# Gated linear attention and a gated feed-forward on one core: wider array tiles for nine chunks, twelve products fewer, another written order

## The chip, the cores and the metric

The kernel runs on one core of a Trainium2 chip. The metric is device time in microseconds (us), the median over runs. The engines are TensorE (PE, with its weight loads shown apart as PEld), VectorE (DVE), ScalarE (ACT), GpSimd (POOL) and SyncE (SP), which only issues transfers here. Each engine works through its own instructions in the order in which the program lists them and waits where an input isn't there.

## The reference

```python
# q, k, v, f_logit: (4, 8, 768, 48)   batch, head, time, head_dim
f = 1.0 / (1.0 + np.exp(-f_logit))
for t in range(S):
    state = f[:, :, t, :, None] * state + np.einsum('bhd,bhe->bhde', k[:, :, t], v[:, :, t])
    y[:, :, t] = np.einsum('bhd,bhde->bhe', q[:, :, t], state)
x = y, heads side by side                      # (4, 768, 384)
h = np.maximum(x @ w_in, 0.0)                  # 384 -> 1024
conv = sum over k of conv_w[k] * h shifted by k - 1 in time
out = (h * sigmoid(conv)) @ w_out              # 1024 -> 384
```

The attention is a linear recurrence with a decay per row of the state. The feed-forward takes its output, convolves the hidden layer over three steps in time for a gate, and projects back.

## The kernel before

**Chunks.** Time is cut into chunks of 128, six per batch, 24 in all; chunk n is batch n // 6. The eight heads stand as four pairs, one head on partitions 0 to 47 and one on 64 to 111. In a chunk the recurrence becomes products. Two exponentials of the summed gate logarithm (`decays`, tile fi and fd) scale k and q (`scaled_k`, `scaled_q`). `scores` multiplies them into a 128x128 triangle per head (PSUM tile pa) and DVE copies it under a mask (am). `turned` transposes k (ptk, then kp). `state` forms the rank update of the state from kp and v (pk) and decays the state. `values` adds the masked scores times v and the old state times q (py), and writes a high and a low half for the feed-forward (xT). Products in plain fp32 leave two records each in the trace, one for each pass.

**Scores and rank updates.** `scores` (L328) cuts the triangle into 32-row strips and leaves out the part above the diagonal: for each pair and each strip two products, one per head, with 48 rows and 32 weight columns; the moving side is 128, 96, 64 or 32 columns long. That is 32 products per chunk. `state` (L343) cuts each head's update in two halves of 32 columns: 16 products per chunk, with 128 rows, 32 weight columns and 64 moving columns. The last chunk of a batch has no update.

**Feed-forward.** It works on half batches of 384 time steps (unit u), in single-pass products (fp32r) of high and low halves: three per pair of blocks. `hidden` makes one of eight blocks of 128 hidden channels: 9 products into ph, ACT and DVE for the gate's argument; `gated` the gate; `result` splits 128 rows into gh and gl (ACT L468, DVE L470) and makes 24 products into po. The weights come as 64-bit numbers and are turned into high and low halves on the chip by POOL, ACT and DVE (`single`, `split`).

**The order.** Nothing is scheduled by a program. Every function is a generator that yields after each step, and the string ORDER (L25 to L78) names which generator makes its next step. A token's letter is the function: F, L, M, V load gate logarithms, k, q and v (SP); x is the gate (ACT, twice), G its sum (PE for the first six chunks, DVE later), p the decays (ACT), t the last decay (POOL), K and Q the scaled k and q, a the scores (PE, then DVE's mask), k the transpose (PE, then ACT), s the update (PE, DVE, POOL), y the values (PE, PE, ACT, DVE). I and O load weights, J and P widen them, H and S split them; c is the convolution's weights; h, m and j are the hidden layer, r the result, z and b a closing check. Behind the letter is the chunk, the block or unit and block. For one engine only the order of its own steps counts, so the order of a token among those of other engines matters through the waits alone. SP's loads stand in one queue as well: a load that waits for its buffer holds back those behind it. The gate logarithms have two buffers of three chunks (tag "fb"), so F6 to F8 wait for G0 to G2.

**Zero products.** `warm` (L528) is token w: 12 products of 512 columns in fp32r, from two places of the split weights that are set to zero at the start (L164 to L166), into a PSUM buffer that nothing reads. In the order they stand around r0.0 to r0.2:

```
S7 S7 m2.4 j1.4 j1.4 m1.6 m2.4 m2.4 m1.6 h2.4 m2.5 G11 r0.0 r0.0 r0.1 V12 r0.0 m2.4 r0.0 s9 r0.0 w w y9 s9 p11 w w s9
r0.0 m1.7 p11 w x12 w w w w w Q11 y9 a10 m1.1 m2.7 w m1.0 r0.1 L12 r0.1 r0.1 r0.1 m1.7 m1.1 K11 j1.6 m1.1 m1.0 r0.2 j1.6
V11 m2.7 m2.7 y10 m2.7 j1.0 s10 y10 a11 r0.2 w y10 s10 m2.6 h2.6 m2.6 m2.5 j1.0 r0.1 m2.0 M12 m2.2 r0.2 y10 m2.1 m2.0
```

(An r token makes its casts and subtractions first and then a quarter of its products at each of four further tokens.)

Of the kernel before, what the change touches and what calls it, by code (L numbers as in the profile page):

```python
# [30 lines left out]
J1.1 K4 P3 p5 k3 O5 J1.1 t4 H2.1 J1.1 m0.0 m0.3 K5 P0 G6 Q4 m0.0 P3 y3 p5 m0.3 F11 y3 h0.2 M5 F9 P3 m0.1 H1.1 m0.1 y3 M6  # L31
P0 p6 V6 L7 m0.0 P3 s3 K6 P3 M7 H0.1 H0.1 s3 P5 m0.1 s3 P0 V4 O2 P0 a4 m0.2 m0.2 m0.2 H1.1 a4 h0.4 m0.6 m0.0 S3 p7 y3
m0.1 S3 m0.3 k4 x8 m0.0 m0.1 P0 m0.2 F10 x8 m0.3 k4 P0 Q5 m0.6 p6 P2 K7 G8 a5 t6 m0.5 m0.5 x9 s4 y4 s4 m0.2 P5 x9 Q6
m0.5 y4 m0.4 y4 m0.5 m0.4 P5 a5 S0 m0.6 m0.2 m0.1 y4 k6 O1 P2 a6 m0.4 S0 m0.3 m0.6 m0.5 s4 P2 y5 t5 y5 p8 O6 P5 P5 m0.4
k6 m0.5 P5 m0.7 y5 m0.7 m0.7 m0.1 k7 m0.2 M8 y5 p7 Q7 m0.4 t7 P2 P1 k7 M10 m1.1 m1.0 a6 j0.2 s6 m0.0 p8 m0.5 O4 t8 S5 P2
M9 j0.0 y6 m1.0 G9 m1.1 P1 L8 m0.4 s6 y6 j0.0 m0.7 m1.1 a7 m1.2 m0.7 h1.0 m1.1 P1 m1.2 a7 m1.2 m1.4 F12 Q8 P2 m0.4 y6
m0.6 K8 m0.6 P1 V7 m1.0 m1.4 j0.4 y7 L9 k8 m1.0 S2 m1.5 y7 m1.5 p9 j0.4 L11 j0.2 L10 G10 S5 P4 F14 F13 h1.2 P4 k8 m1.4
K9 h1.4 m1.2 s7 x12 p9 m0.6 m1.5 m1.3 m1.4 V8 m1.3 m1.3 t9 a8 m1.7 P1 m1.5 m0.7 P1 m0.7 L13 m1.6 m1.3 P6 y7 P4 s7 m1.6
S1 P4 k9 P4 m1.5 m1.6 k9 s7 j0.6 m1.2 O7 a8 m1.7 p10 y7 s8 S2 j0.6 P4 K10 y8 Q9 y8 m1.3 s8 m1.7 h1.6 a9 y8 y8 m1.7 m1.7
P7 m1.2 k10 m2.3 P6 m1.2 m1.3 P6 m2.2 S1 m1.6 P7 k10 m2.3 V9 P7 m1.3 p10 r0.0 P6 P6 j1.2 m2.3 m2.5 a9 s8 m1.6 t10 S4 P6  # L40
m1.0 j1.2 r0.0 S4 P7 m2.3 V10 m2.2 m1.4 m1.4 P7 m1.4 M11 m1.5 m2.5 m2.2 h2.2 m2.5 Q10 S6 y9 P7 m2.2 y9 r0.1 m1.5 a10 S6
S7 S7 m2.4 j1.4 j1.4 m1.6 m2.4 m2.4 m1.6 h2.4 m2.5 G11 r0.0 r0.0 r0.1 V12 r0.0 m2.4 r0.0 s9 r0.0 w w y9 s9 p11 w w s9
r0.0 m1.7 p11 w x12 w w w w w Q11 y9 a10 m1.1 m2.7 w m1.0 r0.1 L12 r0.1 r0.1 r0.1 m1.7 m1.1 K11 j1.6 m1.1 m1.0 r0.2 j1.6
V11 m2.7 m2.7 y10 m2.7 j1.0 s10 y10 a11 r0.2 w y10 s10 m2.6 h2.6 m2.6 m2.5 j1.0 r0.1 m2.0 M12 m2.2 r0.2 y10 m2.1 m2.0
m2.0 G13 m2.6 G14 m2.1 F15 m2.7 r0.2 p13 K13 t11 k13 m2.1 m2.3 m2.6 r0.5 m2.6 r0.2 r0.2 G12 h2.0 M13 r0.2 r0.2 m2.7 p13
k13 s10 p12 m2.1 p12 r0.5 a11 V13 m2.4 Q13 L14 y11 Q12 y11 K12 a12 m2.0 m2.3 m2.4 r0.5 r0.4 t13 r0.2 r0.4 r0.5 V14 r0.4
F17 F16 y11 r0.5 m2.5 M14 p14 r0.5 r0.4 m2.1 x15 m2.3 y11 x15 k12 r0.1 m3.2 r0.3 p14 t12 k12 K14 m2.7 a12 a13 M15 m2.6
m2.2 m2.1 r0.2 r0.5 m2.2 r0.3 L15 m2.4 y12 s12 m2.0 m3.2 j2.2 m2.1 m2.0 s12 j2.2 r0.4 r0.4 m2.0 L16 k14 m3.3 y12 j2.0
m3.2 r0.4 V15 G15 m2.6 G16 h3.2 p15 k14 m2.5 m3.0 j2.0 m3.3 t14 m3.3 m3.0 M16 m3.2 K15 m3.0 s13 m3.1 m3.1 s13 j2.6 s13
a13 y12 m3.2 h3.0 m3.1 m3.0 k15 m3.3 m3.3 p16 F19 m3.6 K16 m3.6 k15 m3.5 p15 m3.2 G17 m3.6 m3.1 m3.1 Q14 m3.5 m3.5 s14  # L50
j2.4 m3.1 j2.6 r0.5 m3.0 y13 j2.4 h3.6 m3.6 y13 y13 h3.4 p16 a14 s14 a14 r1.0 F20 k16 m3.7 y13 m3.5 r0.3 m3.7 k16 r1.0
Q16 F18 m3.6 L17 m3.7 m3.7 Q15 y14 s15 x18 s14 m3.1 y14 m3.7 m3.5 m3.2 r0.4 a15 r1.0 t15 r1.0 V18 y14 r0.3 m3.7 m3.7 x18
V17 a15 s15 m3.5 m3.4 m3.4 G18 m3.4 r0.3 m3.6 p17 r1.0 r0.3 m3.5 s15 r1.0 M17 p17 m3.4 y14 r1.1 m3.0 K17 m3.0 r0.3 t16
y15 m3.3 L18 r1.0 F23 j3.0 r1.1 F21 V16 m3.4 M19 s16 y15 a16 m3.6 y15 Q17 s16 p18 r1.1 r1.1 a16 K18 m3.4 r1.1 m3.4 r0.3
p18 y15 j3.0 r1.1 m3.3 m4.4 k18 j3.6 F22 m4.7 m4.7 G19 r1.1 m4.5 m4.5 L19 j3.4 m4.4 m4.7 p19 y16 y16 j3.2 a17 j3.4 t17
K19 j3.6 r1.1 m4.4 m4.5 r1.0 s16 h4.6 k18 m4.7 a17 h4.4 m4.4 r1.2 k19 m4.5 y16 j3.2 k19 y16 m4.1 m4.0 t18 h4.0 m4.0 G20
r1.2 h4.2 M18 m4.0 m4.3 m4.1 m4.1 m4.0 m4.1 m4.3 V19 Q18 y17 p19 r1.2 s18 r1.3 r1.3 r1.2 x21 M20 y17 y17 m4.4 a18 L20
m4.6 m4.2 L21 m4.5 Q19 m4.3 m4.6 m4.6 m4.4 x21 a18 m4.2 s18 t19 y17 m4.0 m4.2 s19 m4.0 y18 m4.3 y18 m4.2 y18 G23 a19
m4.3 m4.3 m4.0 m4.6 s19 L22 r1.2 r1.2 m4.5 r1.3 r1.2 m4.2 G21 r1.2 r1.5 r1.3 V22 p20 m4.6 m4.5 r1.2 m4.2 m4.2 r1.3 p20
r1.3 t20 m4.7 r1.3 r1.4 r1.2 M23 r1.5 r1.5 m4.1 m4.4 j4.4 K20 r1.5 Q20 p21 m4.6 m4.6 r1.5 p21 a19 r1.5 m5.5 m4.1 m5.5  # L60
r1.4 m5.5 m4.1 m4.3 r1.5 r1.5 m5.4 r1.3 K21 y19 t21 j4.0 j4.4 y19 a20 p23 k20 j4.0 p23 s19 m5.4 m5.4 M21 L23 r1.4 m4.7
m4.7 j4.2 r1.4 j4.2 Q21 h5.4 k20 a20 r1.4 j4.6 j4.6 m5.4 V20 m5.4 m5.5 r1.4 m5.5 r1.4 m5.7 m5.4 m5.7 m5.1 K23 r2.0 m5.1
m5.1 m5.7 m5.3 m5.3 h5.6 y19 m5.3 r2.0 r2.1 k21 y19 m5.4 m5.7 h5.0 r1.4 m5.0 m5.0 h5.2 m5.0 m5.5 m5.1 k21 m5.3 m5.6 m5.6
m5.3 m5.2 G22 m5.2 m5.2 m5.6 p22 m5.7 m5.0 r2.0 y20 m5.7 m5.3 m5.5 m5.7 m5.0 r2.1 s20 s20 M22 y20 j5.4 a21 m5.6 r2.0 V21
m5.3 r2.1 y20 m5.6 y20 j5.4 a21 t23 m5.6 s20 r2.0 m5.0 m5.0 r2.0 p22 Q22 m5.6 r2.1 j5.6 j5.6 r2.1 K22 r2.1 h6.6 s21 m5.1
m5.1 m5.2 h6.4 y21 t22 y21 Q23 r2.1 m5.2 a22 r2.0 r2.2 m6.4 m6.5 s21 m6.1 m5.2 m6.4 r2.0 m5.2 m6.4 m6.5 m5.1 m6.1 m6.5
j5.2 a22 s21 j5.0 j5.0 m6.4 h6.0 m6.6 z m6.6 k22 m6.5 m6.1 y21 r2.2 m6.0 m6.1 j5.2 m6.0 m6.6 m6.7 r2.2 r2.5 m6.7 m6.7
m6.4 k22 r2.2 m6.4 y21 m6.5 m6.0 y22 m6.4 m6.5 m6.5 s22 y22 m6.6 r2.5 a23 s22 r2.2 y22 m6.6 m6.6 r2.2 r2.1 r2.2 r2.2 a23
m6.1 m6.0 m6.7 m6.7 r2.5 r2.3 s22 r2.5 m6.1 y22 m6.2 V23 r2.2 m6.3 r2.5 m6.0 m6.1 j6.4 m6.7 m6.0 r2.5 m6.0 r2.4 j6.0
r2.3 m6.3 m6.2 m6.3 m6.7 m6.2 h6.2 m6.6 r2.5 j6.6 y23 m6.3 j6.0 y23 y23 y23 r2.3 j6.4 m6.3 r2.3 m6.2 m6.3 r2.2 r2.3 j6.6  # L70
r2.3 m6.2 r2.3 m6.3 m7.7 h7.6 m6.2 m7.1 m7.1 z m7.7 m7.7 m7.1 m7.0 h7.0 m7.7 m7.0 r2.4 m7.2 m7.1 m7.1 m7.0 m7.2 m7.1
m7.0 m7.4 m7.0 r2.3 m7.2 h7.4 m7.4 m7.4 m6.2 j6.2 m7.4 j6.2 m7.5 h7.2 m7.1 m7.5 m7.2 m7.2 m7.2 m7.0 m7.0 m7.4 m7.5 m7.4
m7.3 m7.3 m7.7 m7.6 m7.6 m7.3 m7.5 m7.7 r3.0 r3.0 m7.6 m7.3 m7.3 r2.4 m7.5 j7.0 m7.7 r2.4 r2.4 m7.6 m7.3 m7.5 r2.4 m7.5
m7.3 r3.0 r3.1 m7.4 m7.2 r3.0 r3.1 j7.2 j7.2 r3.0 r2.5 m7.6 r3.0 r3.1 r3.0 r3.0 r3.2 j7.0 r3.1 r2.4 r3.1 m7.6 r3.2 r3.2
m7.6 r3.2 r3.1 r3.2 r3.2 r3.2 j7.4 r3.2 r3.2 r3.2 z r3.2 j7.4 r3.2 j7.6 j7.6 r3.1 r3.2 z r3.2 r3.2 r3.2 r3.2 r3.2 r3.2
# [6 lines left out]
def gla_moe_kernel(ctx, tc, q_in, k_in, v_in, f_in, w_in, conv_w, w_out, out):  # L82

    nc = tc.nc
# [243 lines left out]
    def scores(n):  # L328
        kT, qT = raw["k", n], raw["q", n]
        for p in range(NP):  # L330
            for i in range(NB):
# [9 lines left out]
        yield
# [364 lines left out]
```

## Time and profile before

| | us |
|---|---|
| median of the runs shown | 317.6 |
| the runs | 317.25, 317.6, 320.34 |
| the profiled execution | 316.99 |
| its span | 315.3 |
| PE busy | 301.2 (96%) |
| DVE busy | 255.7 (81%) |
| ACT busy | 225.9 (72%) |
| POOL busy | 74.8 (24%) |

The span runs from the first to the last instruction of one execution. Times in the rows are counted from the start of the span. An engine's busy time adds up its instructions; for PE the end of each product is modelled, so a PE that is always busy may still have stalls in it, and what a product takes is read from one start to the next.

### The profile page before, as it was taken

To read this page: it belongs to the slowest core of one execution; us is meant where nothing else is said; L and a number is where in the kernel's file an instruction comes from. 1 tells how busy PE (TensorE), PEld (TensorE's weight loads), DVE (VectorE), ACT (ScalarE), POOL (GpSimd) and SP (SyncE) were. 2 spreads that over 40 slices of the span, in tenths; PEclk is the share of its full clock that TensorE was granted. 3 is DMA by queue.
4 is the path that set the end of the run, shared out by engine and by line. 5 is a ranking of instruction groups with operands and counts; after the bars stand their busy time and mean duration, and the time that the engine had idled before them with its cause. 6 is when DMAs were issued, how large, how long until landed. Compare 5 with 4: busy or idle time off the path is not lost.

```text
span 315.3 us, 10904 instructions
## 1 busy us (share of the span) xinstructions
PE 301.2 (96%) x4747; PEld 276.6 (88%) x4747; DVE 255.7 (81%) x389; ACT 225.9 (72%) x424; POOL 74.8 (24%) x106
## 2 busy tenths in 40 slices
PE   6887899999999999999999999999999999999995
...
PEclk9699999999999999999999999999999999999998
...
GB/s 240 364 282 349 379 266 37 152 266 22 202 4 92 176 154 93 120 201 68 38 166 121 160 71 4 58 152 94 2 0 87 2 27 0 52 1 0 78 52 53
DMA packets 19382, 36.93 MB, mean 117 GB/s; under 512 B 2156, under 2 KB 5252, under 8 KB 19332
## 3 DMA queue, kind: packets, MB, share of 16 engines
...
q8 instruction: 38, 0.62, 0.7%
...
q14 instruction: 12, 0.10, 0.1%
...
## 4 chain that ended last, share of the span: by engine, by line
PE 90%; DMA 3%; ACT 3%; issue 2%; SPq 1%; DVE 1%
PE po L482 32%; PE ph L429 32%; PE py L373 11%; PE pa L336 6%; PE pk L351 3%; PE ptk L321 3%; PE pl L285 2%; DMA fb<-in_f_logit_dram 2%; DMA v<-in_v_dram 1%; PE pz L531 1%; DVE g L450 1%; ACT fb L267 1%; ACT g L448 1%; ACT L448 0%; SPq L259 0%
## 5 line engine op out<-in xcount | busy, mean ns | idle before, releaser
L429 PE MATMUL ph<-xT,wih 128*128 128x384 f32 x384 | 101.8, 345 | 2.5 <-issue 1.5
L429 PEld LDWEIGHTS ph<-xT,wih 128*128 128x128 f32 x384 | 67.1, 188 | 6.4 <-issue 4.2
L482 PE MATMUL po<-woh,gh 128*128 128x384 f32 x192 | 65.0, 339 | 0.0
L429 PE MATMUL ph<-xT,wil 128*128 128x384 f32 x192 | 64.5, 336 | 0.0
L482 PE MATMUL po<-woh,gl 128*128 128x384 f32 x192 | 64.2, 335 | 0.0
L482 PE MATMUL po<-wol,gh 128*128 128x384 f32 x192 | 64.2, 334 | 0.0
L439 DVE SCALAR_TENSOR_TENSOR g<-hb,cw,g 128x384 f32<-128x384 f32 (+1 forms) x64 | 42.1, 669 | 12.9 <-ACT g L437 12.8
L470 DVE TENSOR_TENSOR gl<-g,gh 128x1024 fp32r<-128x1024 f32 (+4 forms) x34 | 31.8, 942 | 12.4 <-ACT gh L468 12.1
L441 DVE SCALAR_TENSOR_TENSOR g<-hb,cw,g 128x384 f32<-128x384 f32 (+1 forms) x64 | 40.7, 652 | 0.5
L432 ACT ACTIVATE hb<-ph 128x384 f32<-128x384 f32 x64 | 30.8, 488 | 13.8 <-PE ph L429 13.7
L437 ACT ACTIVATE g<-hb,cw 128x384 f32<-128x384 f32 (+1 forms) x64 | 38.8, 615 | 0.5
L482 PEld LDWEIGHTS po<-woh,gh 128*128 128x128 f32 x192 | 36.0, 188 | 0.7 <-issue 0.2
L468 ACT CAST gh<-g 128x1024 fp32r<-128x1024 f32 (+4 forms) x34 | 26.7, 804 | 13.2 <-PE po L482 13.1
L482 PEld LDWEIGHTS po<-wol,gh 128*128 128x128 f32 x192 | 36.1, 188 | 0.1
L429 PEld LDWEIGHTS ph<-xT,wil 128*128 128x128 f32 x192 | 36.0, 188 | 0.0
L482 PEld LDWEIGHTS po<-woh,gl 128*128 128x128 f32 x192 | 36.0, 188 | 0.0
L315 POOL TENSOR_TENSOR q<-q,fd 128x512 f32<-128x512 f32 x19 | 26.7, 1406 | 35.8 <-ACT fd L300 21.1
L339 DVE COPY_PREDICATED am<-mask,pa 128x1024 f32<-128x1024 uint8 x24 | 31.9, 1327 | 4.0 <-PE pa L336 3.9
L450 DVE SCALAR_TENSOR_TENSOR g<-g,hb 128x768 f32<-128x768 f32 (+1 forms) x32 | 31.2, 985 | 4.6 <-ACT g L448 4.5
L448 ACT ACTIVATE g<-g 128x768 f32<-128x768 f32 (+1 forms) x32 | 26.9, 844 | 8.9 <-DVE g L441 8.6
L361 POOL TENSOR_TENSOR st<-st,ft_all 128x256 f32<-128x256 f32 x16 | 14.1, 883 | 72.1 <-DVE st L359 72.1
L373 PE MATMUL py<-am,v 128*32 128x128 f32 x768 | 26.5, 280 | 0.1
...
## 6 DMA issues: line engine op xcount, KB each, us to landing
...
```

Of the source, the lines that this page charges most:

```text
L315: (nc.vector if n < QV else nc.gpsimd).tensor_tensor(raw["q", n], raw["q", n], fds[n][1], ALU.mult)
L339: nc.vector.copy_predicated(a_b[n % 2].rearrange("p j (x y) t -> p (j x) y t", y=2), mask, pa.rearrange("p j (x y) t -> p (j x) y t", y=2))
L373: nc.tensor.matmul(py[G * p:G * p + G, t, :], lhs, rhs, start=start, stop=stop)
L429: nc.tensor.matmul(ph, w, xts[b, hf][:, t, xl, :], start=(k == 0), stop=(k == 3 * KT - 1))
L432: nc.scalar.activation(hb[:, 2:HS + 2], ph, AF.Relu, scale=0.5)
L437: nc.scalar.activation(cv, hb[:, 1:n + 1], AF.Copy, scale=cw[:, 1, f:f + 1])
L439: nc.vector.scalar_tensor_tensor(cv, hb[:, 2:n + 2], cw[:, 2, f:f + 1], cv, ALU.mult, ALU.add)
L441: nc.vector.scalar_tensor_tensor(cv, hb[:, 0:n], cw[:, 0, f:f + 1], cv, ALU.mult, ALU.add)
L448: nc.scalar.activation(cv, cv, AF.Tanh)
L450: nc.vector.scalar_tensor_tensor(cv, cv, 1.0, h_b[:, fp:fp + 2, 1:n + 1], ALU.add, ALU.mult)
L470: nc.vector.tensor_tensor(lo, g[:, f:f + k], hi.bitcast(F32), ALU.subtract)
L482: nc.tensor.matmul(po, g[:, f, :], w, start=(i == 0), stop=(i == 3 * NF - 1))
```

## The change

Four edits. For chunks below NA = 9, `scores` makes one product per pair and head: 48 rows, 128 weight columns, 128 moving columns, the whole square, 8 products per chunk. For the same chunks, `state` makes one product per pair and head: 128 rows, 64 weight columns, 64 moving columns, 8 per chunk. Token w, its generator and the two memsets are gone. ORDER is written anew; apart from w it has the same tokens, each as often as before.

```diff
+NA = 9
...
 ORDER = """
-F0 I0.0 F1 c J0.0 x0 x0 L0 G0 M0 x1 F2 I1.0 J0.0 J0.0 p0 x1 L1 V0 c G1 L2 p0 c J0.0 c J0.0 K0 Q0 x2 c c p1 J0.0 a0 c M1
-x2 a0 p1 K1 I2.1 H0.0 k0 F3 c G2 k0 t0 I2.0 H0.0 y0 F7 p2 J1.0 s0 M2 y0 J1.0 J1.0 x3 Q1 J1.0 F4 K2 J1.0 x3 s0 c V1 a1
-J1.0 t1 a1 p2 k1 J2.0 t2 F5 Q2 G3 y0 I0.1 k1 J2.0 x7 x7 k2 k2 s1 J2.0 y0 H1.0 G7 p3 V2 y1 x4 J2.1 J2.1 s1 J2.0 J2.1 J2.0
-H1.0 F6 a2 I1.1 L3 J2.0 y1 y1 x4 p3 J2.1 H2.0 a2 M3 G4 J0.1 J2.1 y1 O3 y2 s1 K3 O0 Q3 J0.1 J2.1 h0.0 x6 J1.1 L4 J0.1 x5
-J0.1 H2.0 L6 s2 F8 y2 a3 y2 s2 J0.1 s2 x5 y2 t3 L5 h0.6 J0.1 H2.1 V3 p4 p4 a3 G5 m0.3 x6 J1.1 m0.0 k3 M4 P3 V5 J1.1 m0.3
...
+F0 x0 I0.0 F1 L0 x0 M1 x1 J0.0 J0.0 J0.0 G0 p0 F3 x1 p0 J0.0 c c J0.0 M0 G1 K0 c L1 c F2 p1 I1.0 Q0 V0 x2 J0.0 J1.0 k0 c
+x2 k0 c H0.0 J1.0 K1 L2 a0 p1 c c J1.0 a0 H0.0 I2.0 G2 t0 y0 p2 J1.0 Q1 J1.0 y0 I2.1 p2 c x3 K2 M2 F7 x3 J1.0 t2 s0 a1
+s0 H1.0 J2.0 V1 F4 J2.1 I0.1 a1 y0 J2.0 k1 k1 F5 G3 Q2 k2 h0.6 L4 J2.1 x7 V2 M3 J2.0 x7 y0 H1.0 x4 k2 y1 J2.0 t1 J2.0 L3
+I1.1 V3 y1 F8 G7 s1 J2.0 J2.1 J2.1 J2.1 J0.1 F6 s1 y1 x4 O0 p3 y1 p3 H2.0 a2 O3 a2 K3 J0.1 O5 s2 s1 M5 Q3 V4 x5 J0.1 G4
+y2 J2.1 J0.1 H2.0 s2 y2 y2 J0.1 a3 x5 M4 y2 H2.1 p4 J1.1 k3 k3 L5 J1.1 H2.1 x8 t3 J0.1 K4 a3 G5 x6 O2 p4 O6 J1.1 x6 J1.1
...
+m2.4 r0.0 j1.4 S6 S7 m1.7 m1.0 j1.4 M11 r0.1 G11 r0.0 M13 r0.0 r0.0 m1.7 m2.5 m1.6 h2.4 m2.4 r0.0 m2.4 t10 r0.0 r0.1 t9
+r0.2 m1.1 m1.0 r0.2 r0.1 m1.1 p11 m1.6 m1.7 p11 x12 y9 r0.1 s9 s9 r0.1 m1.0 m2.7 r0.1 m2.1 y9 m2.1 a10 m2.1 m2.7 j1.0
...
 """
...
-    WARM = 12
...
-    wz, wy = wih[:, KT - 1, DFF - WC:], woh[:, NF - 1, :P]
-    nc.gpsimd.memset(wz.bitcast(F32), 0.0)
-    nc.gpsimd.memset(wy.bitcast(F32), 0.0)
...
     def scores(n):
         kT, qT = raw["k", n], raw["q", n]
-        for p in range(NP):
+        for p in range(NP if n < NA else 0):
+            for j in range(2):
+                r = slice(HP * j, HP * j + D)
+                nc.tensor.matmul(pa[:, j, p, :], kT[r, p, :], qT[r, p, :], start=True, stop=True)
+        for p in range(NP if n >= NA else 0):
             for i in range(NB):
...
         for p in range(NP):
             for j in range(2):
+                if n < NA:
+                    nc.tensor.matmul(pk[HP * j:HP * j + HP, p, :], kp[:, 2 * p + j, :], vt[:, p, j, :],
+                                     start=True, stop=True)
+                    continue
                 for x in (0, G):
...
-    def warm():
-        for i in range(WARM):
-            pz = ps.tile([P, WC], F32, tag="mm", name=f"pz{i}", bufs=MB)
-            nc.tensor.matmul(pz, wy, wz, start=True, stop=True)
-            yield
-
-    todo = {"c": load_cw(), "z": checked(), "b": loaded(), "w": warm()}
+    todo = {"c": load_cw(), "z": checked(), "b": loaded()}
```

On PE, the order of the first chunks changes from G0 G1 a0 k0 c G2 y0 s0 y0 a1 k1 G3 k2 s1 y1 a2 y1 G4 y2 s2 y2 a3 G5 to G0 G1 k0 a0 c G2 y0 y0 s0 a1 k1 G3 k2 y1 y1 s1 a2 s2 G4 y2 y2 a3 k3 G5. From r0.0 on it was r0.0 s9 w (ten) m2.7 w r0.1 m2.7 m2.7 y10 and is, with s9 now ahead, r0.0 m2.4 r0.1 m2.7 m2.1.

## Rows read from the trace of the kernel before

**Rows 1.** Page, the span in 40 slices: PE and the granted clock, in tenths.
```profile
PE   6887899999999999999999999999999999999995
...
PEclk9699999999999999999999999999999999999998
```

**Rows 2.** Windows: us, length, busy PE, PEld, DVE, ACT, POOL, clock, DMA share, GB/s.
```profile
88.00:96.00 8.00, 8.00 (x153) 7.47 (x153) 8.00 (x14) 6.57 (x13) 0.44 (x1) 1.00 0.02 4
...
104.00:112.00 8.00, 8.00 (x182) 7.43 (x182) 6.96 (x11) 6.32 (x12) 1.26 (x1) 1.00 0.53 179
```

**Rows 3.** Timeline of PE around the zero products (pz): start, length, group, count.
```profile
99.07 2.58 PE L531 MATMUL pz<-wih,woh 128*128 128x512 f32 x10
101.49 0.51 PE L429 MATMUL ph<-xT,wih 128*128 128x384 f32 x2
...
102.01 0.40 PE L531 MATMUL pz<-wih,woh 128*128 128x512 f32 x1
102.25 0.33 PE L482 MATMUL po<-woh,gh 128*128 128x384 f32 x1
...
110.42 0.50 PE L531 MATMUL pz<-wih,woh 128*128 128x512 f32 x1
110.75 0.51 PE L429 MATMUL ph<-xT,wih 128*128 128x384 f32 x2
```

**Rows 4.** Timeline of DVE: the subtraction that r0.1's products need.
```profile
98.68 1.20 DVE L470 TENSOR_TENSOR gl<-g,gh 128x1024 fp32r<-128x1024 f32 x1
```

**Rows 5.** Timeline of PE: update, values, scores, transposes of one chunk.
```profile
80.29 0.65 PE L351 MATMUL pk<-v,kp 128*32 128x64 f32 x32
80.76 1.06 PE L373 MATMUL py<-am,v 128*32 128x128 f32 x32
...
83.07 1.00 PE L336 MATMUL pa<-q,k 48*32 48x128 f32 x64
84.00 0.66 PE L321 MATMUL ptk<-ident,k 128*128 128x128 f32 x4
84.41 0.59 PE L429 MATMUL ph<-xT,wih 128*128 128x384 f32 x2
```

**Rows 6.** Timeline: full 128x128 fp32 products of G4 and their loads; the scores' loads.
```profile
26.09 0.97 PEld L285 LDWEIGHTS pl<-tri,fb 128*128 128x128 f32 x8 [1.44 <-ACT fb L267]
26.09 1.16 PE L285 MATMUL pl<-tri,fb 128*128 128x128 f32 x8 [1.17 <-ACT fb L267]
...
83.06 0.80 PEld L336 LDWEIGHTS pa<-q,k 48*32 48x32 f32 x64 [0.25 <-POOL mswo L180]
```

**Rows 7.** Timeline of PE: the rows with idle time put down to issue.
```profile
29.07 0.37 PE L351 MATMUL pk<-v,kp 128*32 128x64 f32 x12 [0.55 <-issue]
...
35.97 0.51 PE L429 MATMUL ph<-xT,wih 128*128 128x384 f32 x2 [0.82 <-issue]
...
42.30 0.63 PE L336 MATMUL pa<-q,k 48*32 48x64 f32 x40 [0.53 <-issue]
...
48.69 0.45 PE L429 MATMUL ph<-xT,wih 128*128 128x384 f32 x1 [0.67 <-issue]
```

**Rows 8.** Windows between and after those stops, and one early stretch; columns as in rows 2.
```profile
29.07:35.90 6.83, 5.70 (x127) 4.94 (x127) 6.83 (x12) 6.22 (x14) 4.77 (x7) 1.00 1.01 371
...
42.30:48.68 6.38, 5.72 (x127) 4.92 (x127) 6.02 (x11) 6.38 (x13) 3.38 (x3) 1.00 0.62 221
48.68:55.00 6.32, 6.31 (x155) 5.00 (x160) 5.03 (x8) 4.12 (x9) 4.50 (x7) 1.00 0.16 47
...
10.20:16.00 5.80, 5.80 (x98) 4.93 (x101) 4.41 (x9) 3.97 (x9) 1.75 (x4) 0.50 0.84 332
```

**Rows 9.** Timeline: ACT ahead of G4's products, and G5's products.
```profile
25.02 0.48 ACT L401 CAST xT<-py 128x384 fp32r<-128x384 f32 x1 [0.63 <-PE py L373]
...
31.26 1.16 PE L285 MATMUL pl<-tri,fb 128*128 128x128 f32 x8 [0.38 <-ACT fb L267]
```

**Rows 10.** Timeline of PE: G1's products, ahead of the stretch at half clock.
```profile
8.89 1.42 PE L285 MATMUL pl<-tri,fb 128*128 128x128 f32 x8 [1.87 <-ACT fb L267]
```

More of the change, by code (lines that the diff above doesn't have):

```diff
@@ L31 @@
[L31 to L75, printed above, removed]
@@ new lines @@
+I1.1 V3 y1 F8 G7 s1 J2.0 J2.1 J2.1 J2.1 J0.1 F6 s1 y1 x4 O0 p3 y1 p3 H2.0 a2 O3 a2 K3 J0.1 O5 s2 s1 M5 Q3 V4 x5 J0.1 G4
+y2 J2.1 J0.1 H2.0 s2 y2 y2 J0.1 a3 x5 M4 y2 H2.1 p4 J1.1 k3 k3 L5 J1.1 H2.1 x8 t3 J0.1 K4 a3 G5 x6 O2 p4 O6 J1.1 x6 J1.1
+p5 m0.3 m0.3 m0.3 s3 F11 P3 J1.1 s2 G6 P3 J1.1 P0 K5 V6 p5 m0.3 h0.0 m0.0 s3 P3 P3 h0.2 m0.0 Q4 H1.1 y3 H0.1 m0.1 h0.4
+P0 x8 P3 m0.1 m0.2 p6 y3 L6 k4 m0.0 t4 H0.1 F10 m0.2 m0.1 H1.1 P0 P3 K6 m0.0 m0.4 a4 P0 O1 m0.0 m0.2 S3 P0 a4 k4 m0.1 p7
+F9 P5 m0.5 P5 y3 P5 Q5 M6 L7 x9 P5 y3 P5 m0.3 S3 p6 m0.4 m0.5 a5 s3 P0 G8 s4 V5 P2 m0.5 Q6 s4 m0.4 y4 m0.1 V7 t6 m0.4
@@ new lines @@
+m0.2 x9 a5 m0.1 L8 K7 y4 m0.6 y4 y4 S0 p8 m0.5 P2 G9 m0.6 m0.5 k6 s4 m0.6 O4 m0.2 S0 M7 y5 y5 m0.0 y5 m0.5 m0.4 a6 P5 y5
+m0.7 m0.7 m0.6 k6 k7 t5 L9 m0.0 p7 m1.1 L10 m0.1 S5 a6 m0.3 k7 m0.5 m1.1 P2 m1.1 m0.2 P1 j0.0 m0.7 S5 p8 m1.0 Q7 m0.7
+j0.0 m0.7 s6 P2 t8 P1 y6 y6 m0.4 s6 M9 a7 P2 a7 M8 m1.0 h1.0 m1.1 m1.0 t7 m0.2 m1.0 m0.3 m1.3 m1.3 P1 O7 F13 P2 K8 V8
+j0.2 m1.3 m1.2 V9 y6 m0.6 m1.2 m1.2 m1.4 m0.4 Q8 S2 m1.4 P4 k8 y7 S2 p9 j0.4 k8 P4 y7 K9 j0.2 P1 P1 a8 j0.4 s7 h1.2 P1
+P4 m0.7 y7 m1.3 m1.5 m1.2 m1.2 p9 P6 P6 s7 G10 m1.4 m1.7 h1.4 m1.7 s7 m1.4 P4 m0.6 a8 k9 m1.5 S1 m1.6 p10 k9 m1.5 y7 F14
```

38 lines of the change are left out of this document (36 added, 2 removed).

## The prediction

> **What bounds the kernel now.** I read the page's slices first. TensorE (PE) is at 9 tenths or more from the sixth slice to the last but one, and the granted clock is down in the second slice [rows 1]. So there are two parts: some 50 us in which PE has gaps and follows VectorE (DVE), the loads and ScalarE (ACT), and after that 260 us in which PE issues almost without a gap, so that every microsecond of PE work is a microsecond of time. The windows then say how much room the second part has. From 88 to 96 us PE and DVE are both busy 8.00 of 8.00 us; from 104 to 112 DVE has 1.04 us free [rows 2]. PE sets the end, but DVE follows within a microsecond or two around 90 to 100 us: what PE saves there it can keep only as far as DVE keeps up. The last views are the timeline of PE, for what an operation really takes (from its start to the start of the next), and its idle times with their releasers, for gaps before 50 us that an order can close.
>
> The profiled execution took 316.99 us, 1.69 more than its span of 315.3. The runs shown are 317.25, 317.6 and 320.34, so it lies 0.6 us below their median. I sum against 316.99.
>
> **Zero products.** Ten issue in a row from 99.07 to 101.49 (2.42 us), one from 102.01 to 102.25 (0.24), one from 110.42 to 110.75 (0.33) [rows 3]: 2.99 us of PE in the packed part. Were they only filling a wait? The next large piece, r0.1's po at 102.25, needs its low part gl, which DVE ends at 98.68 + 1.20 = 99.88 [rows 4]. Without the products PE would be done with s9 at 99.07 and with the three ph at 99.59, so it would wait 0.3 us. The removal is worth 2.99 - 0.3 = 2.7 us. Its ends: 0, if in the new order the gap they filled comes back whole, and 3.0. The two memsets that go are on GpSimd ahead of a load and cost nothing.
>
> **Scores.** A chunk's 32 products are 64 records now (fp32 goes twice); they take from 83.07 to 84.00, 0.93 us [rows 5]. The new form has 8 products, 16 records, each with 128 weight columns and 128 moving columns, in two row halves. No row shows a 48x128 tile, so I bound it. From below: four 128x128 transposes of 128 columns take 84.00 to 84.41, 0.10 us each [rows 5]; if the halves run side by side, 8 deep, that is 0.82 us, 0.1 less than now. From above: a full 128x128 fp32 record of pl takes 1.16 / 8 = 0.145 us [rows 6]; with no overlap of the halves 16 x 0.145 = 2.32 us, 1.39 more. The rows nearest in kind are pl's for the depth and pa's own for the overlap: pl's 8 loads of 128 columns take 0.97 us, 7.6 ns per 8 columns, while pa's 64 loads of 32 columns take 0.80 us, 3.1 ns per 8 columns [rows 6]; so the two row halves do load side by side in pa, and I take 8 x 0.145 = 1.16 us, 0.23 more. Nine chunks: +2.1 us, between -1.0 and +12.5. DVE's copy behind them is unchanged.
>
> Against this stands a rule: the Trainium skill (TensorE: Matmul & The Clock Gate, "LDWEIGHTS") gives a load's time as its columns over 1.2 per ns, however few rows. Both forms load 2048 columns, so by it a chunk would need 1.7 us of loads in either form. The 0.80 us above say that loads of different row halves don't queue; if they do for wide tiles, it is the third rival below.
>
> **Rank updates.** pk's 32 records take from 80.29 to 80.76, 0.47 us [rows 5]. The new form has 16, each 64 weight columns wide, in two column halves. If the halves overlap as the four quarters do now, the depth in moving columns is the same: 0 (at best half, -0.2). If they run one after another, 16 x 0.145 / 2 = 1.16 us, +0.7. I take 0, between -0.2 and +0.7, for each of the eight chunks with an update among the first nine.
>
> **Fewer instructions.** PE stops for 0.55, 0.82, 0.53 and 0.67 us with "issue" named and nothing else [rows 7]. Between one such stop and the next lie 127 products and some 127 loads, three times over, while the DMA engines are 62 to 101% busy; once they are at 16%, 155 products pass without one [rows 8]. So PE's instructions come in blocks, and a block that is fetched among full queues comes late. Chunks 0 to 4 and their four updates lose 5 x 48 + 4 x 16 = 304 records of each kind, 2.4 blocks: two of the four stops go, -1.3 us (from 0 to -2.6). The Trainium skill (Runtime: NRT & Kernel Launch, "Instruction fetch mechanics") has the blocks of 256 instructions, in agreement, but calls the crossing mostly hidden; by that the change would save nothing here and the sum would be 1.3 us higher. The rows show it isn't hidden while loads run.
>
> **Written order.** Counted from the two orders, with the engine of each step from the code. The same steps stand in both, so what can change is gaps. Two close. G4 waits 1.17 us for ACT's second gate step [rows 6], because ACT first waits 0.63 us for y1's products [rows 9]; in the old order a2 (0.93) stands ahead of y1's second half, in the new one behind it: -0.9. G5's gap of 0.38 [rows 9] gets k3 (0.41) in front: -0.4. One opens: in the new order k0 and c come before and after a0, and a0 itself is longer while the clock is at half, so DVE's mask of chunk 0 comes up to a microsecond later. That falls in the part where PE has slack, and DVE has K1 moved in front of it; 0, at most +1. SP's loads: M1 and F3 go ahead of M0 and F2, 512 KB, or 1.4 us at the 371 GB/s of a stretch full of loads [rows 8]. Q0 is behind K0 and J0.0 on DVE, which hide most of it; M2 now goes ahead of F7, which waits for G2's products, so the queue holds 256 KB more while it waits. I take 0. In the packed part, r0.1 follows r0.0 after one group of ph instead of s9, ten zero products and one ph; DVE has 8 steps between the two subtractions instead of 14 (about 4 us less), so it can follow, but without reserve. Order as a whole: -1.3, between -3 and +3.
>
> **Sum.** -2.7 (zero products) + 2.1 (scores) + 0 (updates) - 1.3 (stops) - 1.3 (order) = -3.2: 316.99 - 3.2 = 313.8 us.
>
> **The rivals.**
> - *DVE takes over.* What PE saves before 100 us makes it reach r0.0 to r0.2 earlier, while the number of DVE steps ahead of r0.0's subtraction grows from 113 to 116. DVE has no idle time from 88 to 96 [rows 2]. For it: that row. Against it: the free 1.04 us just behind, and 142 DVE steps instead of 145 ahead of r0.2. Then about 2.2 of the 3.2 us come back as waits of PE on gl: 316.0.
> - *The clock recovers sooner.* From 10.2 to 16 us the granted clock is 0.50, the 1.2 GHz level, after PE had stood idle 1.87 us ahead of G1 [rows 8, 10]. PE does about half the work it could: 2.9 us. What PE does differently in that stretch is a0; if the clock comes back earlier behind it, G2, y0 and what DVE does behind them move up: 313.8 - 2.9 = 310.9. Against it: nothing ahead of G1 changes, so the fall stays.
> - *The halves don't overlap (slower).* Nine chunks of scores at 16 x 0.97 / 8 = 1.94 us (loads in one line) to 2.32 us, six of them in or near the packed part. That is +9.1 to +12.5 in place of +2.1: 320.8 to 324.2. It decides from 0.93 + (2.7 + 1.3 + 1.3) / 9 = 1.52 us a chunk on; above that the change is slower than before. Against it: pa's loads.
> - *The clock falls without the zero products.* One more half-clock stretch like that of [rows 8] near 100 us: 313.8 + 2.9 = 316.7. Against it: PE has no gap there for long.
>
> **How the numbers follow.** Forecast 0.35, DVE 0.28, clock sooner 0.20, no overlap 0.12, clock falls 0.05. The predicted time is the forecast's, 313.8, its own range 312.3 to 315.5 (one gap more or less). The range goes from 309.5 (clock sooner and another microsecond of gaps) to 319.0, which leaves out the third rival and little else. About 1% is what a measurement of this kernel can tell: faster means below 314.4, slower above 320.8. Faster: two thirds of the forecast, all of the clock, a little of DVE: 0.47. Slower: most of the third rival, 0.10. Within: 0.43.
>
> **What would show it.** Right: pa's 16 records in about 1.16 us from start to next start; two "issue" stops instead of four before 50 us; G4's gap gone; po of r0.1 right behind r0.0 with under 0.5 us between; PE packed to the end. Wrong: pa above 1.5 us; a DVE or ACT releaser in PE's waits between 85 and 130 us that adds up to over 2 us; a clock digit below 9 beyond the second slice; or a second slice at 9, which would make it faster than I say.

## The result, and the profile after

The change made the kernel faster: 308.96 us (307.3 to 310.83, four runs) against 317.93 (317.25 to 320.34, four runs), a ratio of 0.9706 [0.9624, 0.9788]. Repeated with the experiments it gave 307.97 against 317.95, 0.9776 [0.9728, 0.9824]. Each ratio compares the executions within 1.5% of the fastest of their kernel, so slower ones count in the medians but not in the ratios. The forecast was 313.8 us with a range from 309.5: the direction was right, the size two to three times too small (3.2 us forecast, 7 to 9 by the two ratios). The profiled execution took 307.3 us, 9.7 less than that of before; its span is 305.6, its mean granted clock 0.998 (before 0.986).

The page's slices, PE and granted clock, in tenths:

```profile
PE   7789999999999999999999999999999999999994
...
PEclk9999999999999999999999999999999999999999
```

PE is packed from the fourth slice on (before from the sixth), and the clock's second slice is at 9 where it was at 6 [rows 1]. Where the 9.7 us lie is read from the first and the last product of the results (po), by the view of one tile; two of its rows for each kernel (duration min/median/max in ns, then the first and last start). Before:

```profile
L482 PE MATMUL po<-woh,gh x192: 331/334/445, 94.2 to 310.7; 128*128 128x384 f32 x192
...
L482 PE MATMUL po<-woh,gl x192: 333/334/347, 94.6 to 311.0; 128*128 128x384 f32 x192
```

After:

```profile
L486 PE MATMUL po<-woh,gh x192: 334/334/443, 87.4 to 301.0; 128*128 128x384 f32 x192
...
L486 PE MATMUL po<-woh,gl x192: 334/334/346, 87.7 to 301.3; 128*128 128x384 f32 x192
```

First po to last: 216.8 us before, 213.9 after. So 2.9 us went behind the first po, and 6.8 ahead of it, in the part in which PE had gaps. What PE has to do ahead of it differs little but for the tiles: s9 (0.47 us) moved in front of the first po, one group of ph (0.52) behind it. Windows over that opening part and within it (columns as in rows 2), before:

```profile
0.00:94.20 94.20, 84.05 (x1769) 69.04 (x1770) 84.82 (x140) 78.15 (x157) 40.96 (x70) 0.96 0.61 214
...
8.00:16.00 8.00, 7.11 (x105) 6.06 (x109) 6.41 (x13) 6.17 (x14) 2.46 (x5) 0.60 0.89 352
16.00:24.00 8.00, 7.07 (x284) 6.07 (x273) 7.72 (x14) 7.47 (x16) 2.78 (x5) 0.97 0.94 292
...
8.00:40.00 32.00, 27.25 (x661) 22.77 (x664) 29.48 (x50) 27.66 (x59) 13.38 (x21) 0.89 0.95 340
```

After:

```profile
0.00:87.40 87.40, 81.40 (x1239) 69.66 (x1240) 82.11 (x140) 78.26 (x156) 43.67 (x68) 1.00 0.66 239
...
8.00:16.00 8.00, 6.42 (x113) 5.47 (x115) 7.64 (x16) 7.71 (x17) 2.44 (x5) 1.00 1.04 400
...
24.00:32.00 8.00, 8.00 (x132) 6.91 (x127) 8.00 (x15) 7.54 (x17) 5.09 (x7) 1.00 1.04 403
...
8.00:40.00 32.00, 29.00 (x461) 24.53 (x463) 31.64 (x55) 31.20 (x68) 16.30 (x25) 1.00 1.04 400
```

PE's idle time ahead of the first po fell from 10.15 to 6.00 us and its busy time from 84.05 to 81.40, although PE has more to do there (wider tiles, below). From 8 to 40 us the loads run at 400 GB/s against 340 before, and DVE is busy 31.6 of these 32 us against 29.5. What PE still waits for ahead of the first po (view of waits: sum, times, longest; the row for the kernel's own warm-up at the very start is left out):

```profile
PE pl L281 <- ACT fb L263: 1.4, 1, 1.4
PE pc L243 <- DVE c L186: 0.6, 1, 0.6
PE py L377 <- DVE xT L407: 0.5, 1, 0.5
PE pk L350 <- DVE st L363: 0.5, 1, 0.5
PE pk L355 <- issue: 0.4, 1, 0.4
PE ptk L317 <- DVE st L365: 0.4, 1, 0.4
```

All four "issue" stops of [rows 7], in which PE waited for nothing that the profile shows, are gone (one of 0.44 us stands at 86.02). So are the waits for ACT of G4 and G5 [rows 6, 9]; only G1's stays, 1.4 us for 1.87 [rows 10]. The pieces of the sum, in PE's timeline (groups of rows that stand next to each other, apart where "..." is):

```profile
24.29 0.94 PE L281 MATMUL pl<-tri,fb 128*128 128x128 f32 x6
...
39.26 1.16 PE L329 MATMUL pa<-q,k 48*128 48x128 f32 x16
40.35 0.62 PE L433 MATMUL ph<-xT,wih 128*128 128x384 f32 x2
...
43.73 0.69 PE L350 MATMUL pk<-v,kp 128*64 128x64 f32 x16
44.35 0.62 PE L433 MATMUL ph<-xT,wih 128*128 128x384 f32 x2
...
91.53 0.51 PE L433 MATMUL ph<-xT,wih 128*128 128x384 f32 x2
91.88 0.33 PE L433 MATMUL ph<-xT,wil 128*128 128x384 f32 x1
92.05 0.33 PE L486 MATMUL po<-woh,gh 128*128 128x384 f32 x1
```

G4's products have no wait in front. A chunk's wide scores take 40.35 - 39.26 = 1.09 us to the next start (0.93 before [rows 5]), a wide update 0.62 (0.47). Between r0.0 and r0.1 there are 0.52 us, all of it ph.

### The profile page after: what moved, and what is told of

It is laid out like the page before. It is cut to its first block, busy times and chain, and to the rows that moved or that the text cites. A ratio compares the mean times of both kernels' runs of the same rounds, so it can differ in the third digit from the quotient of the medians.

```text
span 305.6 us, 9770 instructions
## 1 busy us (share of the span) xinstructions
PE 295.7 (97%) x4175; PEld 275.0 (90%) x4175; DVE 253.7 (83%) x389; ACT 225.0 (74%) x424; POOL 82.3 (27%) x104
## 4 chain that ended last, share of the span: by engine, by line
PE 91%; DMA 5%; ACT 1%; DVE 1%; SPq 1%; issue 0%
PE ph L433 34%; PE po L486 34%; PE py L377 11%; PE pa L336 4%; PE ptk L317 3%; PE pk L355 2%; PE pa L329 2%; DMA fb<-in_f_logit_dram 2%; DMA k<-in_k_dram 2%; DMA wis<-in_moe_w_in_dram 1%; PE pk L350 1%; PE pl L281 1%; SPq L255 1%; DVE fb L286 0%; ACT fb L260 0%
## 5 line engine op out<-in xcount | busy, mean ns | idle before, releaser
L443 DVE SCALAR_TENSOR_TENSOR g<-hb,cw,g 128x384 f32<-128x384 f32 (+1 forms) x64 | 39.1, 629 | 7.5 <-ACT g L441 7.5
L311 POOL TENSOR_TENSOR q<-q,fd 128x512 f32<-128x512 f32 x19 | 28.9, 1520 | 48.8 <-ACT fd L296 35.1
L474 DVE TENSOR_TENSOR gl<-g,gh 128x1024 fp32r<-128x1024 f32 (+4 forms) x34 | 32.7, 974 | 11.0 <-ACT gh L472 10.9
L445 DVE SCALAR_TENSOR_TENSOR g<-hb,cw,g 128x384 f32<-128x384 f32 (+1 forms) x64 | 39.4, 643 | 0.4
L454 DVE SCALAR_TENSOR_TENSOR g<-g,hb 128x768 f32<-128x768 f32 (+1 forms) x32 | 33.2, 1047 | 7.2 <-ACT g L452 7.0
L441 ACT ACTIVATE g<-hb,cw 128x384 f32<-128x384 f32 (+1 forms) x64 | 38.0, 614 | 1.5 <-DVE gl L474 1.1
L365 POOL TENSOR_TENSOR st<-st,ft_all 128x256 f32<-128x256 f32 x16 | 15.8, 987 | 55.1 <-DVE st L363 55.1
L491 ACT COPY ob<-po 128x384 f32<-128x384 f32 x24 | 11.3, 478 | 22.1 <-PE po L486 17.0
```

Source lines behind the costliest of these rows:

```text
L311: (nc.vector if n < QV else nc.gpsimd).tensor_tensor(raw["q", n], raw["q", n], fds[n][1], ALU.mult)
L441: nc.scalar.activation(cv, hb[:, 1:n + 1], AF.Copy, scale=cw[:, 1, f:f + 1])
L443: nc.vector.scalar_tensor_tensor(cv, hb[:, 2:n + 2], cw[:, 2, f:f + 1], cv, ALU.mult, ALU.add)
L445: nc.vector.scalar_tensor_tensor(cv, hb[:, 0:n], cw[:, 0, f:f + 1], cv, ALU.mult, ALU.add)
L454: nc.vector.scalar_tensor_tensor(cv, cv, 1.0, h_b[:, fp:fp + 2, 1:n + 1], ALU.add, ALU.mult)
L474: nc.vector.tensor_tensor(lo, g[:, f:f + k], hi.bitcast(F32), ALU.subtract)
```

## The experiments

The first four kernels ran beside before on one chip, the next four on a second and the last four on a third.

**One part at a time.** Three kernels hold one part of the change or two. *old_nozero* is before without zero products (every token w leaves ORDER too):

```diff
-    wz, wy = wih[:, KT - 1, DFF - WC:], woh[:, NF - 1, :P]
-    nc.gpsimd.memset(wz.bitcast(F32), 0.0)
-    nc.gpsimd.memset(wy.bitcast(F32), 0.0)
...
-    todo = {"c": load_cw(), "z": checked(), "b": loaded(), "w": warm()}
+    todo = {"c": load_cw(), "z": checked(), "b": loaded()}
```

> The old order and the old narrow tiles; only the 12 zero products and their two memsets are gone. Both theories: 2.7 us faster than before, about 315 us, with gaps before 50 us as before. If the zero products held the clock, a granted clock below full appears near 100 us and the gain shrinks to nothing (317 us). If they only filled a wait: 317 to 318 us without a loss of clock.

*old_wide_nozero* is old_nozero with the wide tiles for nine chunks:

```diff
+NA = 9
...
+        for p in range(NP if n < NA else 0):
+            for j in range(2):
+                r = slice(HP * j, HP * j + D)
+                nc.tensor.matmul(pa[:, j, p, :], kT[r, p, :], qT[r, p, :], start=True, stop=True)
...
+                if n < NA:
+                    nc.tensor.matmul(pk[HP * j:HP * j + HP, p, :], kp[:, 2 * p + j, :], vt[:, p, j, :],
+                                     start=True, stop=True)
+                    continue
```

> The old order without zero products, with the wide tiles of the first nine chunks. PE's own work is 9 x 0.16 + 8 x 0.13 = 2.5 us more than with narrow tiles. Theory order (the new order closes the gaps): the stops put down to issue go (-2.6), the work comes on top (+2.5), so about 315 us as without wide tiles, and the early gaps stay. Theory tiles (fewer PE instructions and a full clock at 10 to 16 us are what the change brings): 309 to 311 us.

*new_narrow* is after with narrow tiles:

```diff
-NA = 9
+NA = 0
```

> The new order without zero products, but narrow tiles for all chunks (NA = 0). Theory order: 307 to 309 us, as the changed kernel or 1 to 2 us better for the saved PE work less the stops. Theory tiles: the stops put down to issue are back (four, 2.6 us) and the clock is at half from 10 to 16 us: 313 to 315 us.

And the kernel after once more, unedited, on the same chip:

> The changed kernel once more, as the yardstick beside the others on one chip: 307 to 311 us by both theories; the question is how its clock in the first 20 us differs between executions.

| | median (lowest to highest), us | against before |
|---|---|---|
| before | 317.95 (313.66 to 322.44) | |
| old_nozero | 314.93 (312.75 to 318.23) | 0.9972 [0.9933, 1.0011] |
| old_wide_nozero | 315.4 (311.81 to 317.67) | 0.9948 [0.9893, 1.0002] |
| new_narrow | 315.4 (312.3 to 320.37) | 0.995 [0.9907, 0.9993] |
| after_again | 307.97 (307.29 to 309.65) | 0.9776 [0.9728, 0.9824] |

Two theories stood against each other: that the order closes gaps, and that the tiles bring fewer instructions and a full clock. Neither holds alone. Wide tiles in the old order change nothing against old_nozero, the new order with narrow tiles nothing either, and both together take 7 us off. The traces say why each half fails. new_narrow's waits of PE ahead of the first po:

```profile
PE pl L281 <- ACT fb L263: 2.6, 1, 2.6
PE pk L355 <- issue: 2.5, 1, 2.5
PE py L377 <- issue: 2.5, 1, 2.5
...
PE pa L336 <- issue: 1.1, 1, 1.1
```

and one of its windows:

```profile
24.00:32.00 8.00, 3.58 (x128) 2.87 (x127) 6.25 (x13) 4.50 (x9) 3.11 (x4) 1.00 1.04 405
```

Set this beside after's window of the same time: 128 products and 127 loads here, 132 and 127 there, the DMA engines full in both (1.04), but 3.58 us of PE's time here against 8.00. The equal numbers are no limit by themselves, for before has 203 products in this window and new_na2, below, 170. What limits is how long a block of instructions takes to come, and the trace has that, in the packets of a queue named instruction: 38 of 16 KB in before and in new_narrow, 34 in after, which has an eighth fewer PE records. The view of DMA of new_narrow from 24.17 to 24.20 us holds one (so short a window makes the share meaningless):

```profile
q8 instruction: 1, 0.02, 194.2%
```

Three of them start at 16.30, 24.18 and 30.07 us. The stops end at 18.66, 26.45 and 32.49, 2.3 to 2.4 us behind each. In before four start at 26.68, 33.54, 39.87 and 46.46, and the stops of [rows 7] end 2.2 to 2.4 us behind them. So PE takes its instructions in blocks, as the forecast had it, and these stops are waits for a block, which among full queues starts only 5.7 to 7.9 us behind the one before it (26.68 behind one at 21.00); once before's loads have ended, the next follows after 3.4 us (49.84). The new order's full queues make the stops longer (1.1 to 2.5 us, 6.1 in sum, for 0.5 to 0.8 [rows 7]) unless the tiles are wide. Full queues are not needed for a stop: after's at 86.02 us also ends 2.4 us behind a packet, at a DMA share of 0.21 from 83 to 86 us. And not all of the 7 us is stops: behind the one of 2.46 us new_narrow's granted clock is at 0.57 from 32 to 36 us, and the median of its runs' mean clock is 0.985 where after_again has 0.996.

old_wide_nozero has no such stop, and other gaps (timeline of PE):

```profile
20.99 0.69 PE L351 MATMUL pk<-v,kp 128*64 128x64 f32 x16 [2.17 <-DMA v<-in_v_dram]
21.61 1.75 PE L378 MATMUL py<-am,v 128*32 128x128 f32 x32
23.29 2.08 PE L330 MATMUL pa<-q,k 48*128 48x128 f32 x16
...
27.27 1.16 PE L282 MATMUL pl<-tri,fb 128*128 128x128 f32 x8 [1.17 <-ACT fb L264]
```

It waits 2.17 us for v, whose load stands behind F7 in SP's queue, the clock falls behind that wait (py 1.75 us where 1.08 is usual, pa 2.08 for 1.16), and G4's gap is back. Behind the first po it has one wait that after lacks (view of waits from 93 to 110 us):

```profile
PE po L487 <- DVE gl L475: 0.6, 1, 0.6
```

**Is it the one load?** *old_wide_v1* moves V1 ahead of F7.

```diff
-x2 a0 p1 K1 I2.1 H0.0 k0 F3 c G2 k0 t0 I2.0 H0.0 y0 F7 p2 J1.0 s0 M2 y0 J1.0 J1.0 x3 Q1 J1.0 F4 K2 J1.0 x3 s0 c V1 a1
+x2 a0 p1 K1 I2.1 H0.0 k0 F3 c G2 k0 t0 I2.0 H0.0 y0 V1 F7 p2 J1.0 s0 M2 y0 J1.0 J1.0 x3 Q1 J1.0 F4 K2 J1.0 x3 s0 c a1
```

> The old order without zero products and with wide tiles, with one token moved: the load of v for chunk 1 goes ahead of F7, which stands in SP's queue until G2's products are done. In the run without this move PE stood 2.17 us for that load at 21 us, and then worked at half clock until 25 us. Theory queue (with wide tiles the loads' order is what held the old order back): that wait and the clock's fall behind it go, 309.5 to 311 us median instead of 315.4. Theory spread (the old order is late in many places): under 1.5 us faster, 314 to 315.4.

315.43 us (313.29 to 317.39), 0.9943 [0.99, 0.9986]: nothing. The wait for v is gone (one of 0.84 us put down to issue stands in its place), and the time with it isn't, so the theory of the one queue fell. G1 now waits 1.81 us, the clock is at 0.64 behind it, and loads and DVE are as loose as before:

```profile
8.00:16.00 8.00, 6.85 (x45) 5.81 (x49) 6.28 (x12) 5.74 (x14) 2.22 (x5) 0.64 1.00 396
16.00:24.00 8.00, 7.16 (x152) 6.00 (x142) 6.78 (x12) 6.89 (x15) 2.74 (x5) 0.93 0.87 256
```

**How many chunks need the wide tiles?** If the wait for blocks is what they relieve, only chunks that run among full queues need them. Three kernels vary after. *new_na2*, two chunks wide:

```diff
-NA = 9
+NA = 2
```

> The new order, wide tiles for chunks 0 and 1 only. Theory fetch rate (while loads fill the queues PE gets some 254 instructions per 6 to 7 us, whatever they are): from 8 to 40 us PE then has some 630 products and as many loads, 5 blocks, one per 6.4 us, at the limit; stops put down to issue of 1.5 to 4 us in sum, 310 to 313 us. Theory array (wide tiles matter for the clock or in themselves, not by their count): no stops, time within 1 us of the changed kernel, or the clock falls without stops.

*new_na5*, five chunks wide:

```diff
-NA = 9
+NA = 5
```

> The new order, wide tiles for chunks 0 to 4 only, those that PE works off while loads fill the queues. Theory fetch rate: no stops of note, and chunks 5 to 8 save 4 x 0.16 for scores and 3 x 0.14 for updates, 1.1 us: 306.5 to 307.5 us, a little faster than the changed kernel. Theory array: slower than the changed kernel by 1 us or more.

*new_score5*, wide scores in five chunks and no wide update:

```diff
-NA = 9
+NA = 5
...
-                if n < NA:
+                if n < 0:
```

> The new order, wide scores for chunks 0 to 4, narrow updates for all. Each narrow update takes 0.14 us less of PE than a wide one but 16 more products and loads; up to 40 us that is half a block more, 4.2 blocks in 32 us or one per 7.6 us, still above the 6 to 7 us of a fetch. Theory fetch rate: no stops, 306 to 307 us, the fastest of all. If the limit is nearer to 8 us: stops of 0.5 to 2 us and 308 to 309.

new_na2 took 309.74 us (307.72 to 313.62), 0.9761 [0.9706, 0.9816], with two stops back where narrow chunks meet full queues:

```profile
26.85 0.64 PE L377 MATMUL py<-am,v 128*32 128x128 f32 x16 [0.90 <-issue]
...
32.87 0.65 PE L355 MATMUL pk<-v,kp 128*32 128x64 f32 x30 [0.65 <-issue]
```

From 8 to 40 us it has 573 products where after has 461; new_narrow has 621. new_na5 has 446 and no stop, and took 307.1 us (305.57 to 310.17), 0.9673 [0.962, 0.9726], as counted. It is the fastest kernel here, though what it gains on after (307.97 and 308.96) is less than a measurement resolves. new_score5 took 309.22 (306.68 to 311.89), 0.9718 [0.966, 0.9776], a miss against its expectation. It has no stops from 8 to 40 us with 510 products, so updates need not be wide there. Its clock is at 0.79 from 8 to 16 us, but so is new_na5's, behind a longer wait of G1 (2.79 us for 2.28). What new_na5's profile doesn't have is a wait of 1.93 us at 70.58, put down to ACT, and a clock of 0.83 from 70 to 80 us. That wait ends 2.5 us behind an instruction packet, so it may be a stop like the others; no run separates this.

**The early or the late part of the order?** *new_then_old* takes the new order up to G5 and the remaining steps in their old order, *old_then_new* the reverse; both have wide tiles and no zero products. In the lists one line shows the change-over of each, here against after:

```diff
-... t3 J0.1 K4 a3 G5 x6 O2 p4 O6 J1.1 x6 J1.1
+... t3 J0.1 K4 a3 G5 h0.0 x6 L6 s2
+p4 m0.3 x6 m0.0 P3 V5 J1.1 m0.3 J1.1 P3 p5 J1.1 t4 J1.1 m0.0 m0.3 K5 P0 G6 Q4 m0.0 P3 y3 p5 m0.3 F11 y3 h0.2
```

> Wide tiles, no zero products, the new order up to the token G5 (about the first 30 us), then every remaining step in the old order. Theory early (with PE's instruction count out of the way, the first 30 us of the order decide, because what starts PE's packed part is set there): 308 to 310 us. Theory late (the new order gains behind 30 us, in the packed part or up to r0.0): 313 to 315 us, as the old order with wide tiles.

```diff
-... J0.1 H2.0 s2 y2 y2 J0.1 a3 x5 M4 y2 H2.1 p4 J1.1 k3 k3 L5 J1.1 H2.1 x8 t3 J0.1 K4 a3 G5 x6 O2 p4 O6 ...
+F8 y2 a3 y2 s2 J0.1 s2 x5 y2 t3 L5 h0.6 J0.1 H2.1 V3 p4 p4 a3 G5 O5 M5 V4 M4 k3 k3 J1.1 H2.1 x8
+K4 O2 O6 J1.1 x6 J1.1 p5 m0.3 m0.3 m0.3 s3 F11 P3 J1.1 G6 P3 J1.1 P0 K5 V6 p5 m0.3 m0.0 s3 P3 P3 h0.2 m0.0
```

> Wide tiles, no zero products, the old order up to G5, then every remaining step in the new one. Theory early: 313 to 315 us. Theory late: 308 to 310 us.

new_then_old took 313.06 us (311.33 to 315.21), 0.9892 [0.9827, 0.9957]; old_then_new 311.41 (310.1 to 313.37), 0.9856 [0.9793, 0.9919]. Against the 315.4 of the old order the early part alone gives 2.3 us and the late part alone 4.0, measured on another chip; both parts together give more than 7. Neither "early" nor "late" holds alone. Their first po starts at 91.1 and 91.4 us, after's at 87.4. The late part also counts behind it: from the first po to the last the three kernels with the old late order and wide tiles take 215.7 to 216.1 us (new_then_old, old_wide_nozero, old_wide_v1), old_then_new takes 213.8 and after 213.9. In each of the three PE waits 0.56 to 0.59 us for gl and 0.4 to 0.6 with issue named. Which single moves carry the rest of the gain stays open.

**The zero products in the new order.** *new_zero* puts the twelve back: ten behind r0.0, one within r0.1, one behind it (the two memsets come back with them).

```diff
+    def warm():
+        for i in range(12):
+            pz = ps.tile([P, WC], F32, tag="mm", name=f"pz{i}", bufs=MB)
+            nc.tensor.matmul(pz, wy, wz, start=True, stop=True)
+            yield
```

> The changed kernel with the 12 zero products put back, ten behind r0.0, one inside r0.1, one behind it. PE issues without a gap there, so each is paid in full: 12 x 0.25 = 3.0 us slower than the changed kernel, 310.5 to 312 us, with the same clock. If the products hold the clock: less than 1 us slower, with a higher mean clock.

311.88 us (311.22 to 313.28), 0.9858 [0.9801, 0.9914]: 2.9 to 3.9 above the two medians of after. Its po rows:

```profile
L489 PE MATMUL po<-woh,gh x192: 333/334/445, 89.8 to 306.4; 128*128 128x384 f32 x192
...
L489 PE MATMUL po<-woh,gl x192: 333/334/347, 90.1 to 306.8; 128*128 128x384 f32 x192
```

From first to last 217.0 us, 3.1 more than after: they are paid in full, and the clock in the packed part is at 9 with them and without.

**All chunks wide.** *new_na24* asks for the price alone, where loads don't matter.

```diff
-NA = 9
+NA = 24
```

> The new order with wide tiles for all 24 chunks. Behind 40 us PE has no stops to lose, so the 15 further chunks pay their work: 15 x 0.16 for scores and 12 x 0.14 for updates, 4.1 us: 311 to 313 us. If wide tiles gain by themselves, below 308.

314.92 us (313.5 to 317.63), 0.9971 [0.993, 1.0012]: 6 to 7 above after, where 4.1 were counted. One chunk in the packed part shows what the count lacked. After, narrow there:

```profile
144.49 0.65 PE L355 MATMUL pk<-v,kp 128*32 128x64 f32 x32
144.96 1.06 PE L377 MATMUL py<-am,v 128*32 128x128 f32 x32
145.83 0.78 PE L377 MATMUL py<-q,st 128*32 128x128 f32 x24
146.41 0.99 PE L336 MATMUL pa<-q,k 48*32 48x128 f32 x64
147.33 0.44 PE L486 MATMUL po<-woh,gh 128*128 128x384 f32 x1
```

new_na24, the same chunk:

```profile
146.32 0.69 PE L350 MATMUL pk<-v,kp 128*64 128x64 f32 x16
146.94 1.08 PE L377 MATMUL py<-am,v 128*32 128x128 f32 x32
147.83 0.78 PE L377 MATMUL py<-q,st 128*32 128x128 f32 x24
148.54 1.16 PE L329 MATMUL pa<-q,k 48*128 48x128 f32 x16
149.63 0.44 PE L486 MATMUL po<-woh,gh 128*128 128x384 f32 x1
```

Start to start: update 0.47 to 0.62, scores 0.92 to 1.09, and the values just ahead of the scores 0.58 to 0.71, though they are the same instructions. A wide product behind narrow ones starts 0.13 us late. With that a chunk costs 0.47 us more (147.33 - 144.49 = 2.84, 149.63 - 146.32 = 3.31).

## Why the prediction was right in direction and short in size

**Zero products** (-2.7 forecast): right with the new order. 2.9 us are gone behind the first po, and new_zero gets 3.1 back as loss. The 0.3 us of waiting that I had put against it did not come. With the old late order the removal is worth less: from the first po to the last old_nozero takes 214.9 us and the three wide kernels named above 215.7 to 216.1, only 0.7 to 1.9 less than before, and those three show the wait for gl, at 0.6 us. Alone, the removal measured 0.9972 [0.9933, 1.0011], not clear of noise.

**Scores** (+2.1): right in mechanism, a little dear: 1.09 us a chunk for 1.16, 9 x 0.16 = +1.4. The row halves do overlap, so the slower rival is out; its point of decision was 1.52 us. The Trainium skill (TensorE: Matmul & The Clock Gate, "LDWEIGHTS") would by its columns over 1.2 per ns give 16 loads of 128 columns, one after another, an estimated 1.7 us; the wide scores' 1.09 us say that loads in different row halves run side by side.

**Updates** (0): mis-sized, 0.14 to 0.15 us each and 8 x 0.14 = +1.1; the bound of +0.7 each held. Half the records take a third more time, so the two column halves overlap less well than the four quarters did.

**Fewer instructions** (-1.3, "two of the four stops go"): this is the first step that failed. I counted blocks and gave each the same chance of a stop. What limits is how long a block takes to come while loads run: here it started 5.7 to 7.9 us behind the one before it. Where PE uses its blocks more slowly, all four stops go (2.57 us, and 0.44 come later); where it uses them faster, the stops grow with the load on the queues (6.1 us in new_narrow). By the Trainium skill (Runtime: NRT & Kernel Launch, "Instruction fetch mechanics") crossing a block is mostly hidden; the 2.53 us of one stop in new_narrow say it isn't among full queues, and the 0.44 us of after's stop at 86.02 that it isn't always hidden elsewhere.

**Written order** (-1.3, between -3 and +3): the second. The closed gaps were read rightly: G4's 1.17 and G5's 0.38 us are gone. But I bounded the order by gaps that I could name, as if it and the tile widths added up. They don't: the order keeps the loads at 400 GB/s and DVE at 31.6 of 32 us, which with narrow tiles starves PE of instructions and with wide ones pays in full. Parts that gave 0 each beside old_nozero gave 7 us together, and no sum of parts taken one by one could show that. Inside the order the parts nearly add up (2.3 and 4.0 us). The packed part, which I put at 0 for the order, gave some 2 us of that.

**Clock sooner** (rival, 0.20): its sign, the second slice at 9, came, and its 310.9 is the nearest of the forecasts, but not by its mechanism. It had the clock fall and come back sooner; in the profiled after the clock doesn't fall there at all (1.00 from 8 to 16 us). Before, it is at 0.60 and 0.97 in the two windows from 8 to 24 us: 8 x 0.40 + 8 x 0.03 = 3.4 us of PE's work, the largest piece ahead of the first po that I can name. What it is worth in time is less sure. In new_na5 the clock is at 0.79 from 8 to 16 us and G1 waits 1.4 us longer than in after, and yet its first po starts at 87.4 as after's does, with 1.1 us less work in its tiles. The clock's share varies from run to run: the mean granted clock has a median of 0.984 over 29 runs of before and 0.996 over the runs of after, and in before's runs a thousandth goes with about 0.26 us, so some 3 us of the 9 to 10 are clock (worked out from that line, not isolated by a run).

**DVE takes over** (rival, 0.28): no. PE has one wait from 85 to 130 us, 0.44 for instructions. **Clock falls without zero products**: no, its clock is at 9 to the end.

The terms with their measured sizes ahead of the first po (+2.5 wide tiles, -2.1 stops, -1.5 G4 and G5, -3.4 clock, -0.5 at G1, -1.9 two waits that only before has, +2.0 the four small waits on DVE shown above) make -4.9 of the 6.8. Of the other 1.9 some 1.1 lie in the order of ph: ahead of the first po PE enters its products from another tile 16 times instead of 22, and its timeline shows 0.1 us more for the first two products behind another tile (40.35 to 40.81 us in after, where the next pair takes from 40.99 to 41.33) and mostly 0.1 more for the last one ahead of one. No run assigns the remaining 0.8. The two waits of before (view of waits; the longer one of the first row, at 85.91 us, ends 2.2 us behind an instruction packet too, so it may be one more stop):

```profile
PE ph L429 <- ACT hb L432: 1.0, 2, 0.7
PE pk L351 <- DMA v<-in_v_dram: 0.9, 1, 0.9
```
